# A windowed attention and feed-forward kernel whose order of operations comes from a table instead of a list scheduler

## The chip, the cores and the metric

The kernel runs on one core of a Trainium2 chip. The core has TensorE (PE in the profile, with its weight loads as PEld), VectorE (DVE), ScalarE (ACT), GpSimd (POOL) and SyncE (SP), each with a queue of its own that is worked off strictly in order, and 16 DMA engines that move what the queues issue. The metric is the time of one execution in microseconds (us), the median of three runs; lower is better.

## The reference, cut to what matters

```python
# attention: 8 batches, 8 heads, 512 local and 32 global tokens, head size 64
s_g  = scale * q_g @ concat(k_g, k_l).T          # 32 global queries see all 544 keys
out_g = softmax(s_g) @ concat(v_g, v_l)
s_ll = where(abs(i - j) <= 32, scale * q_l @ k_l.T, -1e9)
s_l  = concat(scale * q_l @ k_g.T, s_ll)         # 512 local queries: a window and the global keys
out_l = softmax(s_l) @ concat(v_g, v_l)
x = concat(out_g, out_l)  ->  4352 rows of 512
# feed-forward
h = x @ w_in                                     # 512 -> 2048
g = h * erf(softplus(h))
out = g @ w_out                                  # 2048 -> 512
```

## The kernel before

The attention goes head by head. For each pair of heads, TensorE computes the windows' scores (`s`, 64 small matmuls with 64 rows by 32 columns of the array, `scores`); VectorE adds the mask and takes the maximum (`sm`, `mx`), ScalarE takes the exponentials; TensorE transposes the result (`t`, four matmuls of 128x128); VectorE or ScalarE copies it (`pt`); TensorE multiplies it with the values (`o`, 32 small matmuls a head, 64 a pair, 128 rows by 32 columns; `va` and `vb` are the values' windows); VectorE normalizes (`rs`, `xn`). The global queries have a chain of their own (`ga`, `gb`, `gt`, `go`, `gx`). Batch by batch the result goes through DRAM (`xsc`) and comes back as the feed-forward's input (`rx`, split into `xh` and `xl`).

The feed-forward works on 512-token chunks. `h` is a block of 12 matmuls (128x128 against 512 columns; high and low parts of both factors, three products). ScalarE computes softplus and erf of a few blocks at a time, each with its own table load (`gate`), VectorE multiplies and splits (`gh`, `gl`), and `op` (`project`, six matmuls each) adds up the output. The hidden dimension is cut into 8 units; three are worked first for all chunks and their sums wait in DRAM (`part`); the other five follow in the second part, for chunk pairs with a scheme of seven products of blocks (`pa` to `pd`, weights `wq`). The weights come as 64-bit floats that VectorE turns into 32-bit ones (`raw_in`, `top_in`; `raw_l_in`, `raw_out`). At the start TensorE runs fillers (`spare`), matmuls of constants whose result nobody reads.

Everything is written as operations (`Program.add`): what engines can run it and how long that takes, a key that stands for its due time, what it reads and writes. `Program.schedule` (L192) is a list scheduler: it goes through time, keeps the free buffers of every pool, and gives each engine the ready operation with the smallest key. It has terms for the switch between tile shapes (`TURN`, L57), for a limit on TensorE's small instructions in a stretch (`crowded`, L223), for the queue's ring and for fillers. The order that it returns is the order in which the operations are written into the engines' queues and in which the buffers rotate (L1490 on):

```python
CROWD, STRETCH, EVADE = 254, 4.013, 0.444
...
            for at, m in reversed(issued):
                n += m
                if at <= now - stretch:
                    break
                if n > CROWD:
                    t = max(t, at + stretch - now)
```

Of the kernel before, what the change touches and what calls it, by code (L numbers as in the profile page):

```python
# [30 lines left out]
CROWD, STRETCH, EVADE = 254, 4.013, 0.444  # L31
# [26 lines left out]
NEAR = 3.364  # L58
# [77 lines left out]

class Op:
# [3 lines left out]
class Program:  # L141
# [46 lines left out]
    def filler(self, dur, fn, heat, since, before):  # L188

        self.idle = (dur, fn, heat, since, before)  # L190

    def schedule(self):  # L192
        free = {}
        ready = {e: [] for e in self.LAT}
        until = dict.fromkeys(self.LAT, 0.0)
        events, order, now, bus = [], [], 0.0, {"SP": 0.0, "ACT": 0.0}
        line, front = sorted(self.ops, key=lambda o: o.key), 0

        def push(op):
            for e in op.ways:  # L200
                heapq.heappush(ready[e], (op.key, op.seq, op))

        def elsewhere(op, e):

            for o, dur in op.ways.items():
                if o != e and dur < op.ways[e]:
                    wait = max(0.0, until[o] - now)
                    wait += sum(i[2].ways[o] for i in ready[o] if i[:2] < (op.key, op.seq) and i[2].eng is None)
                    if wait + dur < BIAS * op.ways[e]:
                        return True  # L210
            return False

        for op in self.ops:
            for b in op.new:
                free[b.pool, b.tag] = b.bufs - MORE.get(b.tag, 0)
            if op.waits == 0:
                push(op)
        heapq.heappush(events, (0.0, -1, 0, None))
        ahead = AHEAD
        fill_dur, fill_fn, fill_heat, since, before = self.idle  # L220
        warmth, issued, ring, mode = [], [], [], "F"

        def crowded(n):  # L223

            t = 0.0
            stretch = LOADED[2] if LOADED[0] <= now < LOADED[1] else STRETCH
            for at, m in reversed(issued):
                n += m
                if at <= now - stretch:
                    break  # L230
                if n > CROWD:
                    t = max(t, at + stretch - now)
                    break
            return t

        def fill():
            nonlocal mode
            dur = fill_dur if now > COLD else 2 * fill_dur
            until["PE"] = max(since, now) + dur
            heapq.heappush(events, (until["PE"], -1, 0, None))  # L240
            if now >= since:
                op = Op()
                op.eng, op.ways, op.fn, op.key, op.start, op.heat = "PE", {"PE": dur}, fill_fn, 0.0, now, fill_heat
                op.new, op.bufs = [], []
                order.append(op)
                warmth.append((now, fill_heat))
                mode = "F"

        taken = []

        def cools():

            return not taken and (now < COLD or now < FILL and sum(h for t, h in warmth[-200:] if t > now - TICK) < HEAT)

        while events or any(o.eng is None for o in self.ops) and ahead < 1e3:
            if not events:
                ahead *= 1.25
                heapq.heappush(events, (now, -1, 0, None))
            now = events[0][0]
            while events and events[0][0] <= now:  # L260
                _, _, kind, op = heapq.heappop(events)
                if kind == 2:
                    push(op)
# [1303 lines left out]
```

## Time and profile before

| what | value |
|---|---|
| median of 3 runs | 898.65 us (898.58 to 901.54) |
| profiled execution, from its first to its last instruction | 900.1 us |
| TensorE busy | 882.4 us, 98% |
| VectorE busy | 688.3 us, 76% |
| ScalarE busy | 549.8 us, 61% |
| mean granted clock of TensorE | 0.996 |

A row's idle time is what its engine waited just before it, and the name behind `<-` is what came last. "issue" is time in which the engine waited for nothing that the profile shows. A matmul's row overlaps the next one's, so the start of the next row tells how long one holds the engine.

### The profile page before, as it was taken

The page shows a single profiled execution, that of the slowest core. Times are in us where ns is not written, and L with a number is a line of the kernel's source. Part 1 is how long each engine was busy: PE and PEld are TensorE (multiplying, and loading weights), DVE is VectorE, ACT ScalarE, POOL GpSimd, SP SyncE. Part 2 cuts the span into 40 slices and gives each one's busy share as a digit, 9 for nine tenths or more (in the row PEclk, how much of TensorE's full clock was granted, in tenths as well). Part 3 has the DMA queues.
Part 4 walks back from the last instruction along what each step waited for, and adds up shares of the span by engine and source line. Part 5 has one row for each costly group of instructions (what it writes and reads, how often), then busy time and mean ns, then how long its engine had stood idle before and what let it go on. Part 6 is the DMA issues. An engine that isn't in the chain of part 4 may idle for free.

```text
span 900.1 us, 22151 instructions
## 1 busy us (share of the span) xinstructions
PE 882.4 (98%) x8781; PEld 717.2 (80%) x8789; DVE 688.3 (76%) x1839; ACT 549.8 (61%) x948; POOL 0.9 (0%) x5
## 2 busy tenths in 40 slices
PE   8899899999999999999999999999999999999998
PEld 4677777777877888888888888888888888888986
DVE  6898998999999978978598987587555956456443
ACT  5588866885588746854564865456524654455660
POOL 0000000000000000000000000000000000000000
PEclk9999999999999999999999999999999999999999
DMA  9898798799788948368676528444393435435222
GB/s 322 293 294 293 267 301 301 257 306 320 265 273 286 313 132 281 105 239 277 213 249 202 178 69 269 164 119 151 108 279 102 134 114 176 146 93 171 75 78 70
DMA packets 120063, 186.43 MB, mean 207 GB/s; under 512 B 14104, under 2 KB 57624, under 8 KB 119960
## 3 DMA queue, kind: packets, MB, share of 16 engines
q1 hardware_dynamic: 119960, 185.02, 62.9%
q8 instruction: 69, 1.13, 0.5%
q14 instruction: 34, 0.28, 0.1%
HBM read 143.56 MB, written 41.42 MB: 206 GB/s over the span
## 4 chain that ended last, share of the span: by engine, by line
PE 88%; DVE 6%; DMA 2%; issue 2%; ACT 1%; SPq 1%; DVEq 0%; ACTq 0%
PE op L398 40%; PE h L398 10%; PE pd L398 7%; PE pc L398 7%; PE pa L398 7%; PE pb L398 3%; PE o L398 3%; PE t L399 3%; PE s L398 3%; DVE sm L410 2%; PE h_g L398 2%; PE gt L399 1%; PE go L398 1%; PE ga L398 1%; DMA k<-in_qk_dram 1%
## 5 line engine op out<-in xcount | busy, mean ns | idle before, releaser
L398 PE MATMUL op<-wouth,gh 128*128 128x512 f32 x544 | 214.8, 395 | 0.0
L398 PE MATMUL op<-wouth,gl 128*128 128x512 f32 x544 | 211.9, 390 | 0.0
L398 PE MATMUL op<-woutl,gh 128*128 128x512 f32 x544 | 211.9, 389 | 0.0
L401 ACT ACT_TABLE_LOAD x105 | 134.7, 1283 | 2.6 <-PEq L1554 0.7
L398 PEld LDWEIGHTS op<-wouth,gh 128*128 128x128 f32 x544 | 102.1, 188 | 21.5 <-issue 0.6
L398 PEld LDWEIGHTS op<-wouth,gl 128*128 128x128 f32 x544 | 102.1, 188 | 21.5
L398 PEld LDWEIGHTS op<-woutl,gh 128*128 128x128 f32 x544 | 102.2, 188 | 20.0
L410 DVE TENSOR_TENSOR gl<-sp,gh 128x512 fp32r<-128x512 f32 x136 | 91.2, 685 | 19.6 <-PE op L398 16.0
L400 ACT ACTIVATE gh<-sp 128x512 fp32r<-128x512 f32 x67 | 42.0, 631 | 100.7 <-PE op L398 91.4
L400 ACT ACTIVATE sp<-sp 128x512 f32<-128x512 f32 x136 | 76.0, 621 | 0.5
L410 DVE CAST gh<-sp 128x512 fp32r<-128x512 f32 x69 | 28.6, 421 | 55.3 <-PE op L398 54.9
L410 DVE CUSTOM_DVE_ANT_0 sm<-s,msk 128x128 f32<-128x128 f32 x256 | 57.1, 285 | 17.3 <-PE s L398 17.2
L398 PE MATMUL h<-xh,winh 128*128 128x512 f32 (+1 forms) x168 | 67.0, 399 | 0.0
L398 PE MATMUL pa<-xh_x_B,wq 128*128 128x512 f32 x184 | 63.9, 389 | 0.0
L398 PE MATMUL pd<-xh_ih_T,wq 128*128 128x512 f32 x184 | 63.8, 389 | 0.0
L398 PE MATMUL h<-xh,winl 128*128 128x512 f32 (+1 forms) x168 | 63.2, 376 | 0.0
L398 PE MATMUL h<-xl,winh 128*128 128x512 f32 (+1 forms) x168 | 63.1, 376 | 0.0
L410 DVE TENSOR_TENSOR pair<-u,pc 128x512 f32<-128x512 f32 x46 | 31.4, 683 | 32.9 <-PE pc L398 32.8
L400 ACT ACTIVATE sm<-sm,mx 128x128 f32<-128x128 f32 x120 | 37.4, 394 | 9.1 <-DVE mx L410 9.1
L399 PE MATMUL t<-cs,sm 128*128 128x128 f32 x256 | 39.2, 286 | 3.0 <-DVE rs L410 1.1
L398 PE MATMUL o<-va,pt 128*32 128x65 f32 x768 | 37.8, 222 | 4.2 <-issue 3.5
L400 ACT ACTIVATE pt<-t 128x512 f32<-128x512 f32 x52 | 30.0, 600 | 17.8 <-PE t L399 17.7
(160 smaller groups left out, 1687.9 us busy)
## 6 DMA issues: line engine op xcount, KB each, us to landing
wq<-wq SPq DMA_DIRECT2D x161, 256.0 KB, 3.4
vb<-in_vB_dram SPq DMA_DIRECT2D x64, 325.0 KB, 5.6
qk<-in_qk_dram SPq DMA_DIRECT2D x28, 656.0 KB, 5.9
rx<-xsc SPq DMA_DIRECT2D x26, 512.0 KB, 6.0
va<-in_vA_dram SPq DMA_DIRECT2D x64, 195.0 KB, 5.3
wq<-part SPq DMA_DIRECT2D x47, 256.0 KB, 4.5
part<-os SPq DMA_DIRECT2D x34, 256.0 KB, 3.3
os<-part SPq DMA_DIRECT2D x34, 256.0 KB, 4.2
```

The source lines that it names most:

```text
L398: pe = lambda n, *a, **k: pinned(nc.tensor.matmul(n, *a, **k))
L399: tr = lambda *a, **k: pinned(nc.tensor.transpose(*a, **k))
L400: act = lambda *a, **k: pinned(nc.scalar.activation(*a, **k))
L401: table = lambda name: pinned(nc.scalar.preload_act_table_set(name))
L410: return lambda *a, **k: pinned(f(*a, **k))
```

## The change

`Program.schedule` and its constants' use go. In their place stands a string `ORDER` of 3098 words; a word is the number of an operation in the order in which they were added, with an `a` where ScalarE runs what VectorE could run too, and `w` is a filler. `Program.ordered` reads it word by word.

```diff
+ORDER = """
+w w w 53 54 349 376 348 3 59 314 318 352 4 w w w 1 316 55 56 315 61 w 2 405 w 353 317 w w 321 334 w 57a 58 354 60 w w
...
     def filler(self, dur, fn, heat, since, before):

-        self.idle = (dur, fn, heat, since, before)
-
-    def schedule(self):
...
+        self.idle = fn
+
+    def ordered(self):
+        order = []
+        for word in ORDER.split():
+            if word == "w":
                 op = Op()
...
+                op.eng, op.fn, op.new, op.ways = "PE", self.idle, [], {"PE": 0.22}
+            else:
+                op = self.ops[int(word.rstrip("a"))]
+                op.eng = "ACT" if word.endswith("a") else next(e for e in op.ways if e != "ACT" or len(op.ways) == 1)
+            order.append(op)
+        assert len({id(op) for op in order}) == len(order) and all(op in order for op in self.ops[-3:])
         return order
...
+                held_by += PIECE.values()
...
-                    need = [Q, K, PIECE[n, 0], PIECE[n, 1]]
+                    need = [Q, K, *(PIECE[i, j] for i in range(n + 1) for j in range(2))]
...
-    for op in prog.schedule():
+    for op in prog.ordered():
```

SyncE's queue at the program's start, before and then after (`q` and `k` are queries and keys of head pairs, numbered by the first head; `cs` and `mby` constants; `raw_in` pieces of `w_in` as 64-bit floats):

```order
L402 DMA cs<-in_cst_dram 128x194
L402 DMA q_0_109<-in_qk_dram 128x288
L402 DMA k_0_110<-in_qk_dram 128x416
L402 DMA q_0_109<-in_qk_dram 128x256
L402 DMA k_0_110<-in_qk_dram 128x352
L402 DMA mby<-in_cst_dram 128x128
L402 DMA q_2_120<-in_qk_dram 128x544
L402 DMA k_2_123<-in_qk_dram 128x768
L402 DMA raw_in_2_0_126<-in_w_in_dram 128x512
L402 DMA raw_in_2_1_130<-in_w_in_dram 128x512
```

```order
L378 DMA raw_in_2_0_109<-in_w_in_dram 128x512
L378 DMA k_2_113<-in_qk_dram 128x768
L378 DMA q_4_115<-in_qk_dram 128x544
L378 DMA q_2_117<-in_qk_dram 128x544
L378 DMA raw_in_2_1_120<-in_w_in_dram 128x512
L378 DMA k_0_123<-in_qk_dram 128x352
L378 DMA mby<-in_cst_dram 128x128
L378 DMA k_0_123<-in_qk_dram 128x416
L378 DMA q_0_122<-in_qk_dram 128x288
L378 DMA k_6_177<-in_qk_dram 128x768
L378 DMA q_0_122<-in_qk_dram 128x256
L378 DMA cs<-in_cst_dram 128x194
```

The weights and the second head pair's keys moved to the front, the first pair's pieces and the constants behind them.

VectorE's queue at the program's start, before and then after (`sm` and `mx` are the masked scores and their maximum, `top_in` the weights' conversion):

```order
L410 ISA sm_0_177,mx_0_178<-s_0_0_137,msk 128x128
L410 ISA mx_0_178 128x1
L410 ISA sm_0_177,mx_0_178<-s_0_0_137,msk 128x128
L410 ISA mx_0_178 128x1
L410 ISA sm_1_181,mx_1_182<-s_0_1_138,msk 128x128
```

```order
L386 TENSOR_SCALAR top_in_2_0_165<-raw_in_2_0_109 128x512
L386 SCALAR_TENSOR_TENSOR top_in_2_0_165<-raw_in_2_0_109,top_in_2_0_165 128x512 x2
L386 SCALAR_TENSOR_TENSOR top_in_2_0_165<-winh_2_111,top_in_2_0_165 128x512
L386 TENSOR_SCALAR top_in_2_1_171<-raw_in_2_1_120 128x512
L386 SCALAR_TENSOR_TENSOR top_in_2_1_171<-raw_in_2_1_120,top_in_2_1_171 128x512 x2
L386 ISA sm_2_180,mx_2_181<-s_2_0_125,msk 128x128
```

The conversion of the first two weight pieces, which stood behind the first pair's masks, comes first of all.

TensorE's queue in the third batch's attention, where the scores of the head pair from head 2 of batch 3 (`s_3_2`) stand; before and then after:

```order
L398 MATMUL s_3_2_0_2219<-qk_3_2_2058 32x128 x4
L398 MATMUL s_3_2_1_2220<-qk_3_2_2058 32x128 x4
L398 MATMUL s_3_2_0_2219<-qk_3_2_2058 32x128 x4
L398 MATMUL s_3_2_1_2220<-qk_3_2_2058 32x128 x4
L398 MATMUL h_0_1_1_2257<-xh_0_1_0_1764,winh_0_0_910 128x512
```

```order
L375 MATMUL t_2_3_2085<-cs_75,sm_2_3_1559 128x128 x4
L374 MATMUL s_3_2_0_2094<-qk_3_2_1948 32x128 x4
L374 MATMUL s_3_2_1_2095<-qk_3_2_1948 32x128 x4
L374 MATMUL s_3_2_0_2094<-qk_3_2_1948 32x128 x4
L374 MATMUL s_3_2_1_2095<-qk_3_2_1948 32x128 x4
L374 MATMUL s_3_2_0_2094<-qk_3_2_1948 32x128 x4
L374 MATMUL s_3_2_1_2095<-qk_3_2_1948 32x128 x4
L374 MATMUL s_3_2_0_2094<-qk_3_2_1948 32x128 x4
L374 MATMUL s_3_2_1_2095<-qk_3_2_1948 32x128 x4
L374 MATMUL o_2_2_2131<-va_2_2_1753,pt_2_2_1898 32x65
L374 MATMUL o_2_2_2131<-vb_2_2_1768,pt_2_2_1898 32x65 x2
```

Before, a block `h` followed these scores; now the 64 small matmuls of `o_2_2` and `o_2_3` follow them at once.

## Rows read from the trace of the kernel before

**Rows 1.** Busy time by stage: PE, PEld, DVE, ACT, POOL, clock, DMA share, GB/s.

```profile
0.00:45.00 45.00, 37.81 (x826) 24.55 (x834) 33.48 (x146) 26.10 (x65) 0.94 (x5) 0.96 0.86 308
45.00:90.00 45.00, 42.38 (x1013) 32.51 (x1012) 42.00 (x191) 36.84 (x92) 0.00 (x0) 1.00 0.89 293
90.00:150.00 60.00, 57.02 (x1093) 45.54 (x1092) 54.23 (x203) 46.08 (x102) 0.00 (x0) 0.97 0.85 286
150.00:240.00 90.00, 89.33 (x1606) 71.37 (x1605) 86.64 (x320) 61.05 (x112) 0.00 (x0) 1.00 0.90 294
240.00:395.00 155.00, 154.56 (x1987) 126.06 (x1986) 139.18 (x418) 109.02 (x189) 0.00 (x0) 1.00 0.68 228
395.00:900.10 505.10, 501.29 (x2268) 417.16 (x2266) 332.75 (x567) 270.68 (x392) 0.00 (x0) 1.00 0.51 159
```

**Rows 2.** Chain of waits, its last long piece: start us, us, what.

```profile
850.02 43.56 PE op L398 x192
```

**Rows 3.** TensorE's longest waits: us in total, times, longest us.

```profile
PE o L398 <- issue: 5.8, 6, 2.3
PE s L398 <- DMA k<-in_qk_dram: 1.4, 1, 1.4
PE s L398 <- issue: 1.2, 2, 1.0
PE t L399 <- DVE rs L410: 1.1, 1, 1.1
PE spare L398 <- PEq L1554: 0.8, 1, 0.8
```

**Rows 4.** Timeline of TensorE at two issue gaps: start, us, operation, idle before.

```profile
66.72 0.87 PE L398 MATMUL s<-qk 64*32 64x128 f32 x40
68.61 0.53 PE L398 MATMUL s<-qk 64*32 64x128 f32 x20 [1.02 <-issue]
...
97.83 0.22 PE L398 MATMUL o<-vb,pt 128*32 128x65 f32 x1 [2.27 <-issue]
```

**Rows 5.** Busy time between three issue gaps, with instruction counts.

```profile
68.00:97.80 29.80, 26.01 (x634) 20.11 (x635) 27.12 (x122) 25.16 (x59) 0.00 (x0) 1.00 0.91 312
97.80:147.50 49.70, 49.02 (x888) 39.42 (x888) 45.06 (x166) 36.44 (x74) 0.00 (x0) 0.97 0.81 270
```

**Rows 6.** DMA queues of the page: the instruction queue's packets and MB.

```profile
q8 instruction: 69, 1.13, 0.5%
```

**Rows 7.** Busy time in the two stretches of half granted clock.

```profile
29.98:33.39 3.41, 3.19 (x35) 2.54 (x38) 1.66 (x4) 2.02 (x6) 0.00 (x0) 0.50 1.05 406
98.24:101.66 3.42, 3.42 (x17) 3.42 (x18) 3.37 (x9) 1.51 (x4) 0.00 (x0) 0.50 1.01 395
```

**Rows 8.** Timeline of TensorE: `s` before another shape, `s` before the same.

```profile
159.25 1.16 PE L398 MATMUL s<-qk 64*32 64x128 f32 x64
160.34 0.55 PE L399 MATMUL gt<-cs,pg 128*128 128x128 f32 x3
...
168.28 1.16 PE L398 MATMUL s<-qk 64*32 64x128 f32 x64
169.18 1.06 PE L398 MATMUL ga<-qk 64*32 64x480 f32 x8
```

**Rows 9.** Busy time in the start's loads; the last column is GB/s.

```profile
2.00:10.00 8.00, 7.84 (x143) 3.75 (x145) 1.78 (x16) 2.63 (x9) 0.00 (x0) 1.00 0.93 277
10.00:13.00 3.00, 2.95 (x49) 2.05 (x32) 2.62 (x5) 1.74 (x4) 0.00 (x0) 1.00 1.04 407
```

**Rows 10.** Timeline of the start, TensorE and VectorE.

```profile
5.55 0.88 PE L398 MATMUL s<-k,q 64*32 64x128 f32 x32
...
7.52 0.29 DVE L410 CUSTOM_DVE_ANT_0 sm<-s,msk 128x128 f32<-128x128 f32 x1 [7.52 <-PE s L398]
...
10.28 0.43 DVE L410 TENSOR_SCALAR top_in<-raw_in 128x512 int32<-128x512 int32 x1 [0.98 <-DMA raw_in<-in_w_in_dram]
...
13.87 0.28 DVE L410 CUSTOM_DVE_ANT_0 sm<-s,msk 128x128 f32<-128x128 f32 x1
```

More of the change, by code (lines that the diff above doesn't have):

```diff
@@ new lines @@
+1124 1561 1526 1151 1565 1109a 214 1521 1566 1100 1101 1522 1593 1052 1554 1104 1527a 1159 215 1184 1102a 1162 1110
+1594a 1128 1132 1121 1193 1551 1163 1111 1112 1549a 1164 1113 101 1165 1133 1114 1595 1149 1115 1523 1194 1116 1550
+1125 1596 1134a 1150a 1170 1513 1209 1210 1187 1555a 1152a 1153 1211 1212 1213 1195 1053 1562a 1224 1154 1126 1093
+1127 1166 109 113 1214 1215a 1160 1196 1168 1597 1167 1188 1189 1155a 1156 1157 1197 1198 1190 1199a 1117 1171 1556
+1216 1135 1249 1518 1227 1235 1236 1217a 1172 219 1191 114 1139 1140 115 117 1185 1598 110 1601 1118 116 1161 1192a
@@ new lines @@
+1352 1657 1333 1335 237 238 240 1336 1337 1309 241 1310 1652a 1663 1661 225 1353 1706 1338 1707a 1703 1799 1306 1307
+1308 1623 1624 1614 1311 1670 1312 1635 1313 1354 1802a 1704 1705 233 1636 1708 234 1658 244 1630 1804 1806 1640 1800
+242 243 1631 1803 239 1807 1808 1667 1662a 1811a 1812 1826 1817 1709 1710 1738 1740 1673 1739 1741 1805 1742 1625
+1575a 1715 1671a 1750 1641 1576 1716 1717a 1809a 1637 1638a 1751 1626 1627 1628a 1664 1680 1665a 231 1823 1813a 1743
+1668a 1841 1847 1810 1818a 1712 1822 1713 1674 1675a 1677 1632 1633a 1711a 1814 1815a 235 1669 1666 1642 1752 1688
@@ new lines @@
+2350 2322 2172 2487a 2503 2324 2469 2180 2174 2325 2182 2473 2175 2360 2477a 2504 2183 2326 2475 2188 2478 2368 2365
+2190 2196 2336 2373 2339 2191 2376 2342 2353 2198 2343 2488 2345 2199 2346 2384 2489 2505 2381 2490 2348 2349 2351
+2492 2389 2491a 2354 2506 2352 2361 2357 2521 2392 2369 2377 2385 2494 2355 2356 2358 2507 2522 2359 2393 2362 2508a
+2523 2396 2399 2370 2493 2402 2378 2495 2496 2498 2497 2524 2386 2499 2525 2509 2394 2397a 2395 2511 2398 2526 2510
+2405 2513 2512 2527 2363 2514 2542 2371 2379 2387 2406 2515 2400 2409 2403a 2517 2401 2543 2404 2516 2528 2418 2544
@@ new lines @@
+2983 2815 2811a 2816 2818 2817 2984 2827 2819 2985 2708 2975a 2989 2976 2829 2843a 2846a 2844 2833 2977a 2990 2847
+2978 2854 2685 2991 2979 2693 2701 2709 2835 2849 2850 2852a 2686 2855 2992 2858 2828a 2861 2694 2830 2864 2831 2834
+2688 2702 2832a 2996 2836 2980a 2696 2689 2837 2981 2704 2697 2839 2853 2997 2838 2705 2874 2840 2998 2879 2867 2882
+2887 2710 2895 2890 2856 2712 2857 2875 2859 2713 2868 2898 2860 2871 2883 2862 2865a 2863 2891 2866 2903 2906 2899
+2986 2869 2870 2872 2876 2873 2987 2884 2988 2999 3003 3004 2907 3005 2892 2910 2913 2900 2916 2993 2908 2911a 2909
@@ L137 @@
+2967 2961 2954 2969 2962 2971 2970 2972
+"""
 class Op:
```

254 lines of the change are left out of this document (103 added, 151 removed).

## The prediction

> **What bounds the kernel now.** I read the table by stage first [rows 1]: stage less TensorE's busy time is its idle time. From 150 us on that is 0.67 us (150 to 240), 0.44 us (240 to 395) and 3.81 us (395 to the end), nearly all of this last at the very end: the chain of waits finishes with 192 `op` matmuls back to back in 43.56 us, 0.227 us each [rows 2], and what follows them is an addition and the output's transfer. So behind 150 us TensorE is the bound and nearly full. Before it the picture differs: 7.19 us idle up to 45 us, 2.62 us from 45 to 90, 2.98 us from 90 to 150. So what a better order can win as idle time, if the end stays, is 7.19 + 2.62 + 2.98 + 0.67 + 0.44 = 13.9 us of 900.1. VectorE is the second queue: 42.00 of 45, 54.23 of 60, 86.64 of 90 us [rows 1]; what TensorE waits for in these stages mostly passes through it.
>
> The list of TensorE's waits says what the idle time is [rows 3]: 5.8 us before `o` and 1.2 us before `s` are "issue", no engine and no transfer being late; 1.4 us are the keys' load and 1.1 us a VectorE operation. The two largest issue gaps lie *inside* an operation, in the middle of a row of small matmuls: 1.02 us after 40 of the 64 of an `s`, and 2.27 us inside an `o` [rows 4]. From just before the end of the first gap to just before the end of the second TensorE shows 634 matmuls and 635 weight loads, 1269 in all, which is 5 x 256 less 11; from there to the next such gap, at 147.5, 888 + 888 = 1776, 7 x 256 less 16 [rows 5] (waits on semaphores are instructions too and are not in these counts). The instruction queue moved 69 packets, 1.13 MB, so 16 KB each [rows 6]. I read this as TensorE's program arriving in pieces of 256 instructions, and a gap as a piece that came late because the piece before it, full of small matmuls, was used up too fast while the data queues were busy.
>
> The Trainium skill, "Runtime: NRT & Kernel Launch", section "Instruction fetch mechanics", says the sequencer refills in 16 KiB blocks of 256 instructions, which the rows agree with, and that crossing such a boundary is mostly hidden, which the gap of 2.27 us contradicts. By that rule the fetch term below would be nothing and the sum -5.3 us instead of -7.9 us.
>
> The granted clock fell to half twice, for 3.41 and 3.42 us, the second right behind the gap of 2.27 us [rows 4, 7]. At half clock TensorE loses half of the stretch, so 1.7 us each.
>
> **The change, part by part.** The operations are the same; 47 fillers (`spare`) stand in both programs. The two edits beside the table make the second half of the first scores, and the operations that share their `q` and `k`, wait for all the pieces of that load. I put that at 0: TensorE reaches them behind ten fillers at the start, and the bytes, worked out below, come later than that wait by themselves. On all queues the last part is word for word the same: 368 of 759 TensorE operations, and what VectorE, ScalarE and SyncE have beside and behind them. In the trace of before this part begins at 394.8 us on TensorE and within 2 us of it on the others. The last 505.1 us are therefore taken as they are, 501.29 us of them busy [rows 1], and the term is 0. What would have to go wrong is a product's weights (`wq`) or a gated tile arriving late because the first part ended earlier; queue share there is 0.51 [rows 1], so I put 0 with a bound of +2 us.
>
> *Turns of TensorE between tile shapes.* An `s` of 64 matmuls followed by `ga` (same 64*32 tiles) holds TensorE from 168.28 to 169.18, 0.90 us; the same `s` followed by the 128*128 transposes `gt` from 159.25 to 160.34, 1.09 us [rows 8]. The difference, 0.19 us, is one turn. I counted turns over the whole list of TensorE's operations (tiles 64*32 for `s` and `ga`, 128*32 for `o` and `go`, 128*128 for the rest): 140 before, 125 after, among them 13 directly from `s` to `o` where there were 2. Fifteen turns at 0.19 us are 2.9 us; at two thirds of that, since an `s` to `o` turn is not in the rows and may cost more than the average, 1.9 us. I take -2.3 us.
>
> *The start.* SyncE now issues first a piece of `w_in` (128 x 512 of 8 bytes, 524 KB), then `k` (393 KB) and two `q` (279 KB each); the scores that come first are those of heads 2 and 3 and need these 1475 KB. The load of before began to move at about 2 us and ran at 277 GB/s until 10 us and at 407 GB/s after [rows 9], so the first scores can start at 2 + 1475/277 = 7.3 us, where they start at 5.55 us now [rows 10]: 1.75 us later. Those of heads 0 and 1 need all of 3128 KB: 2216 KB by 10 us, the rest by 12.3 us, 6.7 us later than now. On the other side VectorE, which now begins at 7.52 us with these scores [rows 10], has its first weights at 2 + 524/277 = 3.9 us; the 3.6 us of weight conversion that stood between the masks of two head pairs (10.28 to 13.87 us [rows 10]) lie before the scores. For the queue that the start waits for, that is 3.6 - 1.75 = 1.9 us won if the pairs' order does not matter. From the waits of [rows 3] that are not "issue" (13.9 us less 7.0 of issue and 0.8 before the first instruction, so 6.1 us) a longer distance between a head's scores and its transposes should take some: in the median the work that TensorE has between them goes from about 9 to about 13 us, priced in the same way as the pieces below. Start and waits together: between -6.1 us (all gone) and +6.7 us (the whole delay of heads 0 and 1 shows); I take -3.0 us, nearer to the lower end since the delay is one pair's and its place is taken by another's.
>
> *Work that changes its engine.* 69 copies and scalings go from VectorE to ScalarE and 66 the other way, so of VectorE's 1236 operations three go. In each stage ScalarE has more free time than VectorE (36.84 against 42.00 of 45 us, 61.05 against 86.64 of 90 [rows 1]), and which copy stands where decides only how soon a TensorE operation is released. Its own term is 0; what it does is part of the waits' -3.0 us, whose bounds hold for it.
>
> *The pieces of the program.* The old scheduler keeps TensorE from issuing more than 254 small matmuls in 4.013 us; the table does not: behind `s_3_2` follows `o_2_2` at once, 128 + 128 instructions in about twice 0.90 us [rows 8]. That sounds as if more pieces would come late. But a piece boundary falls somewhere into such a bunch and the rest of each piece is dense `h` or `op` work: priced with the shortest rows of each operation, the shortest pieces take 3.2 us after and 3.4 us before; under 4.02 us are nine after, five of them at the start, and five before. So I expect the 7.0 us of issue gaps to stay between 4 and 10 us. The piece that ended in the 2.27 us gap becomes 0.9 us longer, and the half clock behind it should go: -0.9 - 1.7 = -2.6 us. Bounds: -7.0 - 3.4 = -10.4 us, and +3.0 us plus two more half-clock stretches, +6.4 us.
>
> *Sum.* -2.3 - 3.0 - 2.6 = -7.9 us. Against the profiled execution 900.1 - 7.9 = 892.2 us. Its span alone is 1.45 us above the median of the runs shown, 898.65 us; taken off that median the change gives 890.75 us. I say **891 us**, 0.85% faster.
>
> **Rivals.**
> 1. *What is won is lost at the same place.* The start's delay (+1.75 us on the first scores, up to +6.7 us on the first pair) eats the waits that go, and gaps for program pieces appear elsewhere at the old size. Then only the turns remain, -2 us at most: 896 to 899 us. For it: nine short pieces instead of five, and a busy start. Against it: the waits in [rows 3] have single causes that another order can avoid.
> 2. *Nearly all idle time goes.* 13.9 us of idle, less the 0.8 us before the first instruction, 3.4 us of clock loss and 2.3 us of turns: at most 18.8 us. Two thirds of it, 12.5 us, would give 886 us, all of it 880 us. For it: the distance between producer and consumer grows throughout. Against it: the start is limited by bytes, as worked out above.
> 3. *Slower: the bunches starve TensorE.* The bunches come where the queues are 0.85 to 0.90 busy, up to 240 us, and 0.68 behind [rows 1]. If each of the 11 new `s`-to-`o` bunches has a gap of 1.0 us (the smaller row of [rows 4]) and one in three is followed by a half-clock stretch, 11 + 4 x 1.7 = 17.8 us are added, less 5.3 us of turns and waits: +12.5 us, 911 us. It decides (+4.5 us) from 0.3 us a bunch on. Against it: a bunch holds 256 instructions, so it always spans two pieces, each with several us of dense matmuls.
>
> **How the numbers follow.** My forecast, between 885 and 894, has 0.51; rival 1 (894 to 903) 0.21; rival 2 (878 to 885) 0.17; rival 3 (over 903) 0.11. The likeliest one's own range is 885 to 894 us. For 8 in 10 I take the range from 881 us, where two thirds to all of the idle time would be gone, to 901 us; below it lie about 0.07 and above it 0.13 (rival 3 and the end of rival 1). A measurement of this kernel tells about 0.5% from no change, 4.5 us: faster means under 894.2 us, which is my forecast and rival 2, with 0.68; rival 1 lies within 0.5%, 0.21; slower than 903.1 us is rival 3, 0.11.
>
> **What would show it.** In the profile after: the stages up to 150 us should hold 5 to 8 us less idle time of TensorE in the same work, and from the operation that stood at 395 us on the same 505 us should follow; if that part is longer, the term 0 was wrong. The first scores should start at about 7.3 us and the first `top_in` on VectorE at about 4 us. The "issue" sum should be 4 to 10 us; above 12 us rival 3 is right. One half-clock stretch or none behind 45 us; if there are three or more, the clock term has the wrong sign. The forecast is wrong in its core if TensorE's idle sum up to 395 us is not lower than 13.9 us.

## The result and the profile after

The changed kernel takes 907.5 us in the median of four runs (904.7 to 908.02); the kernel before, beside it, 899.01 us. The ratio is 1.0081, with a 95% interval of 1.0062 to 1.0100: 0.8% slower, where 0.85% faster was forecast. In a second set of six runs it was 905.18 us, ratio 1.0064 (1.0045 to 1.0083). The profiled execution of the first set is the shortest of its four, 904.7 us with a span of 902.2 us, so the traces of before and after differ by only 2.1 us in span. Other traces of both programs, below, show more.

The stages of the changed kernel, in the columns of [rows 1]:

```profile
0.00:45.00 45.00, 33.45 (x838) 21.98 (x853) 32.36 (x143) 27.57 (x68) 0.94 (x5) 1.00 0.77 289
45.00:90.00 45.00, 42.93 (x945) 32.96 (x934) 42.86 (x181) 37.98 (x98) 0.00 (x0) 1.00 0.89 302
90.00:150.00 60.00, 59.01 (x1227) 47.64 (x1204) 58.49 (x214) 53.42 (x118) 0.00 (x0) 1.00 0.91 300
150.00:240.00 90.00, 87.15 (x1631) 70.37 (x1629) 83.56 (x308) 60.26 (x120) 0.00 (x0) 1.00 0.85 272
240.00:395.00 155.00, 151.54 (x1912) 124.51 (x1911) 142.68 (x425) 106.52 (x185) 0.00 (x0) 0.99 0.72 238
395.00:902.20 507.20, 503.39 (x2277) 418.89 (x2276) 334.71 (x571) 269.97 (x391) 0.00 (x0) 1.00 0.51 159
```

TensorE's idle time up to 395 us is 11.55 + 2.07 + 0.99 + 2.85 + 3.46 = 20.9 us, against 13.9 us in [rows 1]. By the prediction's own last sentence it was wrong in its core. Two stages got better, 45 to 90 and 90 to 150 us; the first got worse by 4.4 us, and the two that had been full by 2.2 and 3.0 us.

TensorE's longest waits, as [rows 3]:

```profile
PE s L374 <- DMA q<-in_qk_dram: 5.6, 1, 5.6
PE o L374 <- issue: 3.0, 4, 0.9
PE pa L374 <- issue: 1.9, 1, 1.9
PE go L374 <- issue: 1.3, 1, 1.3
...
PE op L374 <- DVE gl L386: 0.6, 1, 0.6
```

The largest wait is at the start, on a load. The gaps without a visible releaser sum up to about as much as before, but one of them stands before `pa`, the first of the seven-product blocks, where no row of before had a wait.

The start, in the order of time on TensorE, VectorE and ScalarE, as [rows 10]:

```profile
4.23 0.43 DVE L386 TENSOR_SCALAR top_in<-raw_in 128x512 int32<-128x512 int32 x1 [4.23 <-DMA raw_in<-in_w_in_dram]
...
7.84 1.96 PE L374 MATMUL s<-k,q 64*32 64x128 f32 x64 [5.63 <-DMA q<-in_qk_dram]
...
9.00 0.43 DVE L386 TENSOR_SCALAR top_in<-raw_in 128x512 int32<-128x512 int32 x1 [2.08 <-DMA raw_in<-in_w_in_dram]
9.46 1.42 DVE L386 SCALAR_TENSOR_TENSOR top_in<-raw_in,top_in 128x512 int32<-128x512 int32 x2
...
9.64 0.63 ACT L376 ACTIVATE msk<-mby 128x512 f32<-128x512 uint8 x1 [3.43 <-DMA mby<-in_cst_dram]
...
10.80 0.28 DVE L386 CUSTOM_DVE_ANT_0 sm<-s,msk 128x128 f32<-128x128 f32 x1
```

The first scores start at 7.84 us (7.3 was forecast) and the first conversion at 4.23 us (4 was forecast). What the forecast left out is in the last four rows. In VectorE's queue the conversion of the second weight piece stands ahead of the first mask; its `raw_in` comes at 9.0 us, after 2.08 us without work, and the conversion holds VectorE until it masks at 10.80 us. And every masked score needs `mby`, a load of 66 KB that now stands behind 2.2 MB of others and lands at 9.6 us; what ScalarE makes of it is there at 10.27 us. So VectorE masks first 3.3 us later than in [rows 10], although the scores came only 2.3 us later. The granted clock, too, becomes full later: at 11.5 us, where it was 6.1 us before, and the first 64 matmuls of `s` took 1.96 us, against 1.16 us in [rows 8].

The place of the wait before `pa`, on TensorE and in SyncE's queue (the middle row issues three loads; that of `wq0_0_3_0`, which `pa` reads, is the second of them):

```profile
356.29 0.41 SPq L378 DMA_DIRECT2D wq<-wq  x1
356.75 7.54 SPq L378 DMA_DIRECT2D raw_out<-in_w_out_dram  x2
...
372.64 1.46 SPq L378 DMA_DIRECT2D wq<-wq  x3
...
376.56 0.39 PE L374 MATMUL op<-wouth,gl 128*128 128x512 f32 x1
378.87 0.47 PE L374 MATMUL pa<-xh_x_B,wq 128*128 128x512 f32 x1 [1.92 <-issue]
```

The load is issued at 373.1 us. From 368 to 380 us the view of the transfers has, as median time from issue to landing in its last column:

```profile
wq<-wq SPq DMA_DIRECT2D x6, 256.0 KB, 5.7
```

That gives 378.8 us, and `pa` starts at 378.87, having been free to start at 376.95: 3.8 us of lead for a transfer of 5.7 us. Behind the wait the granted clock falls to half; the busy times of that stretch:

```profile
380.18:383.59 3.41, 3.41 (x10) 2.64 (x9) 3.27 (x7) 3.38 (x6) 0.00 (x0) 0.50 0.84 291
```

### The profile page after: what moved, and what is told of

Same layout as the page of the kernel before. It is cut to its first block, busy times and chain, and to the rows that moved or that the text cites. A ratio compares the mean times of both kernels' runs of the same rounds, so it can differ in the third digit from the quotient of the medians.

```text
span 902.2 us, 22144 instructions
## 1 busy us (share of the span) xinstructions
PE 877.5 (97%) x8779; PEld 716.4 (79%) x8789; DVE 694.7 (77%) x1834; ACT 555.7 (62%) x975; POOL 0.9 (0%) x5
## 4 chain that ended last, share of the span: by engine, by line
PE 78%; DVE 10%; DMA 5%; ACT 5%; issue 2%; SPq 0%; DVEq 0%; ACTq 0%
PE op L374 36%; PE pa L374 7%; PE pd L374 7%; PE pc L374 7%; PE h L374 6%; PE pb L374 3%; PE s L374 2%; PE o L374 2%; PE t L375 2%; PE h_g L374 2%; DMA rx<-xsc 1%; DVE sm L386 1%; ACT L377 1%; DVE xn L386 1%; PE go L374 1%
## 5 line engine op out<-in xcount | busy, mean ns | idle before, releaser
L374 PEld LDWEIGHTS op<-wouth,gl 128*128 128x128 f32 x544 | 102.5, 188 | 22.8 <-DVE gl L386 1.0
L374 PEld LDWEIGHTS op<-wouth,gh 128*128 128x128 f32 x544 | 102.5, 188 | 20.9 <-ACT pt L376 1.0
L386 DVE TENSOR_TENSOR pair<-u,pc 128x512 f32<-128x512 f32 x46 | 31.4, 683 | 32.7 <-PE pc L374 32.6
L374 PEld LDWEIGHTS pa<-xh_x_B,wq 128*128 128x128 f32 x184 | 34.5, 188 | 9.5 <-issue 2.3
L374 PEld LDWEIGHTS pd<-xh_ih_T,wq 128*128 128x128 f32 x184 | 34.5, 188 | 7.2
```

Of the source, the lines that this page charges most:

```text
L374: pe = lambda n, *a, **k: pinned(nc.tensor.matmul(n, *a, **k))
L386: return lambda *a, **k: pinned(f(*a, **k))
```

## Experiments

To compare traces in the same work, I took for each of the 712 real TensorE operations the median time from its start to the next one's start in the trace of before, by its kind and the next one's tile shape. The sum over the operations ahead is "the work done"; an operation's start less that sum is how far TensorE is *behind* the work (fillers count as no work). It grows with every wait, filler and half-clock stretch. The table holds it where 40, 100, 340 and 380 us of work are done and near the end (860), in us, with the times of all runs against the kernel before. The places 340 and 380 enclose the wait before `pa`.

| run | behind at 40 | 100 | 340 | 380 | 860 | median us | ratio (95%) |
|---|---|---|---|---|---|---|---|
| before | 22.2 | 28.6 | 33.2 | 33.2 | 33.3 | 899.0 | |
| e13, before again | 21.9 | 26.9 | 31.5 | 31.5 | 31.6 | 899.88 | 0.9996 (0.9980–1.0013) |
| changed kernel | 25.8 | 27.2 | 30.2 | 34.8 | 34.9 | 907.5 | 1.0081 (1.0062–1.0100) |
| e0, changed again | 25.9 | 29.9 | 33.3 | 38.5 | 38.6 | 905.18 | 1.0064 (1.0045–1.0083) |
| e1, two loads exchanged | 26.3 | 27.6 | 33.0 | 34.8 | 35.7 | 904.39 | 1.0049 (1.0031–1.0068) |
| e4, loads sorted | 25.5 | 27.4 | 31.9 | 32.6 | 33.3 | 903.05 | 1.0042 (1.0025–1.0060) |
| e2, late part old | 25.9 | 28.1 | 48.0 | 48.0 | 48.4 | 919.48 | 1.0219 (1.0196–1.0242) |
| e3, start old | 20.5 | 26.9 | 30.9 | 33.8 | 33.9 | 906.15 | 1.0065 (1.0044–1.0087) |
| e5, start old, sorted | 21.3 | 28.9 | 32.4 | 32.8 | 33.4 | 903.48 | 1.0040 (1.0024–1.0056) |
| e7, VectorE +16 copies | 26.8 | 30.9 | 38.0 | 41.1 | 41.1 | 908.08 | 1.0091 (1.0072–1.0110) |
| e8, sorted, VectorE lighter | 26.6 | 28.3 | 31.2 | 31.5 | 31.6 | 902.02 | 1.0027 (1.0014–1.0041) |
| e9, before, VectorE lighter | 19.6 | 22.8 | 25.5 | 25.5 | 25.6 | 897.65 | 0.9979 (0.9961–0.9996) |
| e10, k and q first | 24.7 | 26.1 | 30.0 | 31.6 | 32.6 | 904.15 | 1.0046 (1.0026–1.0066) |
| e11, fillers first | 24.4 | 28.0 | 30.2 | 31.0 | 31.8 | 902.75 | 1.0040 (1.0022–1.0058) |
| e12, start by need | 26.0 | 27.6 | 31.3 | 31.8 | 32.6 | 903.75 | 1.0041 (1.0018–1.0063) |
| e15, start by need, cs too | 28.0 | 30.2 | 33.5 | 34.1 | 35.1 | 904.8 | 1.0064 (1.0042–1.0086) |
| e14, first part old, sorted | 22.0 | 28.8 | 35.4 | 36.0 | 36.9 | 903.63 | 1.0042 (1.0025–1.0059) |

Not shown is e6 (953.77 us). The traces of one and the same program differ by 1.7 us (before) and 3.7 us (changed) at the end, so single traces tell apart only what is larger, or a wait that is there or not.

**The changed kernel again (e0).** No edit.

> The changed kernel once more, as the base of the experiments, with a second trace. Its four runs spread from 904.7 to 908.0 us and the trace is of the shortest; the other three had spans 3 to 4 us longer. Late-weights theory (the loss is made between 370 and 385 us, where the first product pa waits 1.9 us for weights and the clock halves behind it): a longer run shows longer waits there, by 2 to 4 us. Start theory (the loss is the first scores' delay of about 5.8 us at 14 us): a longer run shows the extra in the first 75 us. Piece theory (issue gaps): the issue sum is 10 us or more in a longer run, against 7.3 us.

Its trace is 3.7 us longer. The wait before `pa` is there again with 1.9 us, with 1.1 us before an `op` for `gl` and one half-clock stretch; between 340 and 380 us of work it falls back by 5.2 us, the first trace by 4.6 us. That is the same loss in both. The extra of the longer run lies elsewhere, mostly between 80 and 100 us of work, so no theory had its place; two issue gaps, of 0.9 and 1.3 us at 111 and 117 us, are most of it.

**Two loads exchanged (e1).** 1820 is the load of `wq0_0_3_0`, 1827 is `pa`, 1826 the load of `wq3_0_3_0`, which is needed later:

```diff
-1662a 1811a 1812 1826 1817 1709
+1662a 1811a 1812 1820 1817 1709
...
-1758 1718 1845 1820 1827 1689
+1758 1718 1845 1826 1827 1689
```

> The changed kernel with two words of its table exchanged: the load of wq0_0_3_0, which stands right before its product pa_0_3_0, takes the place of the load of wq3_0_3_0, which stands 150 words before its product. Nothing else moves. Late-weights theory: the wait of 1.9 us before pa goes and the half-clock stretch behind it (1.7 us) too, so 3.6 us less than the changed kernel, about 904 us, and no new wait of more than 0.5 us before the late wq3. Start theory and piece theory: no change, 907 to 908 us.

TensorE's waits from 335 to 460 us:

```profile
PE pa L374 <- DVE c L386: 0.9, 1, 0.9
PE pc L374 <- DVE c L386: 0.6, 1, 0.6
PE op L374 <- DVE gl L386: 0.3, 1, 0.3
```

The wait of 1.9 us and the half clock are gone: the load's place made the wait. For the half clock that is less certain, since e3 has the wait without it. But 2.7 us came back behind it (33.0 to 35.7 in the table), 1.8 us of them in waits for VectorE. In the time only 0.8 us are left, within the uncertainty.

**All fourteen loads sorted (e4).** The loads' words in the table's order, one line before and one after; their places stay:

```diff
-1826 1823 1841 1847 1822 1821 1845 1820 1842 1824 1844 1825 1843 1846
+1820 1822 1821 1823 1824 1841 1825 1826 1842 1843 1844 1845 1846 1847
```

> The changed kernel, with the 14 loads of the first two products' weights (wq0 to wq6 of 0_3_0 and 0_3_1) put into their 14 places in the order in which TensorE needs them. Late-weights theory in its first form (only the order of these loads is wrong): the whole 4.6 to 5.2 us that the two traces of the changed kernel lose between 340 and 395 us go, about 901 us. Late-VectorE theory (the exchange of two loads alone gave back 2.6 us in waits for VectorE's c, since VectorE is filled there by conversions that the table put off): the same waits of 0.5 to 1 us come again, 903 to 905 us.

Its stages up to 395 us, and the sum over the span:

```profile
0.00:45.00 45.00, 34.11 (x842) 21.84 (x850) 32.34 (x142) 27.45 (x68) 0.94 (x5) 1.00 0.80 289
45.00:90.00 45.00, 43.36 (x924) 32.81 (x905) 42.33 (x179) 37.47 (x96) 0.00 (x0) 1.00 0.87 298
90.00:150.00 60.00, 57.33 (x1160) 46.56 (x1165) 58.02 (x213) 52.51 (x118) 0.00 (x0) 1.00 0.89 299
150.00:240.00 90.00, 87.34 (x1627) 70.33 (x1628) 83.17 (x302) 60.45 (x120) 0.00 (x0) 1.00 0.83 268
240.00:395.00 155.00, 153.36 (x2015) 126.68 (x2005) 143.84 (x432) 108.19 (x187) 0.00 (x0) 1.00 0.74 244
...
sum 900.60, PE 877.00 PEld 715.37 DVE 694.46 ACT 555.62 POOL 0.94; mean PE 146.17 PEld 119.23 DVE 115.74 ACT 92.60 POOL 0.16
```

TensorE's waits from 335 to 460 us:

```profile
PE op L374 <- DVE gl L386: 0.4, 1, 0.4
PE pc L374 <- DVE c L386: 0.3, 1, 0.3
```

Between 340 us of work and the end it now loses 1.4 us instead of 4.7 and 5.3. In the time it is 903.05 us, 2.1 us under e0 and 4.5 us under the first set; its interval and that of e0 overlap, so the size in the time is less certain than the wait in the trace. That leaves 3.1 us to the kernel before.

**The late part in the order of before (e2).** From the 300th TensorE operation on, all that is left stands in the order of before:

```diff
-1597 1167 1188 1189 1155a 1156 1157 1197 1198 1190 1199a 1117 1171 1556
+83 127 129 132 1645 1646 103 105 1647 106 1518 110a 1552a 1553
```

> The changed kernel's table up to its 300th TensorE operation (about 279 us in its trace); from there all that is left stands in the order of before. Late-weights theory: the waits between 370 and 385 us (0.55 + 1.9 + 1.7 us) go and the 2.4 us that the middle had gained stay: span about 898, time about 900 us. Start theory: the start's loss stays whole, 905 to 908 us. Piece theory: 904 to 908 us, since the gaps up to 279 us stay.

The first row of TensorE's waits:

```profile
PE t L375 <- ACT sm L376: 13.9, 2, 12.0
```

This is TensorE's longest wait in that trace (total, times, longest). All three theories missed: 919.48 us. The loss is at the cut, where VectorE and ScalarE first work off what the old order had behind them by then, and TensorE waits 12.0 us in one piece. Behind the cut, from 280 us of work to the end, this trace loses 0.5 us: the old order of the late part has no wait of its own.

**The start in the order of before (e3, and e5 with sorted loads).** What stands ahead of the 120th TensorE operation is put into the order of before:

```diff
-w w w 53 54 349 376 348 3 59 314 318 352 4
+4 3 0 314 315 316 317 w 318 w 1 w w 348
```

> The operations that the changed kernel's table has before its 120th TensorE operation (about 77 us) stand in the order of before; the rest of the table stays. Late-weights theory: the first scores come 2 us earlier again, but the two traces stand within 1 us of each other at 75 us in the same work, so the time stays within 1.5 us of the changed kernel, 906 to 908.5 us. Start theory: 4 to 6 us less, 902 to 904 us. Piece theory: issue gaps of this part go back to those of before, 1 to 2 us less.

> Both edits at once: what stands before the 120th TensorE operation in the order of before, and the 14 weight loads in the order of need. If start and weights are lost independently: 901 us less what the start is worth, 899 us or less. If the start's 5 us are given back by 100 us whatever its order (as the trace with the old start shows: 20.5 against 25.8 us behind the work at 40 us of it, 26.9 against 27.2 at 100), it equals the run with the sorted loads alone within 2 us.

At 40 us of work they are 5.3 and 4.2 us ahead of the same table with the new start, at 100 us no more than 0.3 ahead, and at the end within 1 us; 906.15 and 903.48 us. I first read that as a start that is given back whatever its order. The waits of e3 from 45 to 100 us say otherwise:

```profile
PE s L374 <- ACT pt L376: 2.7, 2, 2.0
```

They stand just before the cut at 77 us (e5: 2.8 us), and e2 shows what a cut can cost. So these two runs don't tell whether the start matters.

**The start without a cut (e10, e11, e12, e15).** All on the sorted loads. The first words of the table, changed, then in e10, in e12 and in e15 (349 and 348 are `k` and `q` of heads 2 and 3, 314 to 318 those of heads 0 and 1, 1 is `mby`, 0 is `cs`, 53 and 59 are `raw_in`); e11 only moves twelve fillers of the changed kernel's own start, ten ahead of the first scores and two right behind them.

```diff
-w w w 53 54 349 376 348 3 59 314 318 352 4 w w w 1 316 55
+w w w w w w w w w w 349 348 1 3 4 2 352 w w 353 354 53 54 376
...
+w w w w w w w w 349 348 1 314 318 316 315 317 3 4 2 352 w w 353
...
+w w w w w w w w 349 348 1 0 314 318 316 315 317 3 4 2 352 w w 353
```

> On the kernel with the sorted weight loads: SyncE issues k_0_2, q_0_2 and the mask mby first and raw_in behind them, VectorE masks the scores of heads 2 and 3 before it converts the first weights, and 12 of the 47 fillers stand ahead of and right behind these scores. Nothing else moves, so there is no seam. By bytes the scores can start at 2 + 672/277 = 4.4 us (7.84 us in the changed kernel), the first masked score at about 6 us (10.80 us). Start theory (what the changed order has lost against before, apart from the weights, is its start: 5.6 us of wait for q and a cold clock until 11.5 us): 3 to 5 us less than 903.05, so 898 to 900 us. Theory that a start's gain is given back by 100 us: 902 to 904 us.

> On the kernel with the sorted weight loads: only 12 of the 47 fillers move, ten of them ahead of the first scores, where TensorE waits for q anyway. The granted clock should be full before 7.84 us instead of from 11.5 us, so the first 64 scores take about 0.9 us instead of 1.96. Start theory: 1 to 1.5 us less, 901.5 to 902 us. Theory that the first masked score waits for mby (landed at 9.6 us) and not for the scores: no change, 903 us.

> On the kernel with the sorted weight loads: SyncE issues k and q of heads 2 and 3, the mask mby, then all of k and q of heads 0 and 1, and only then raw_in and q_0_4; VectorE masks these heads before it converts weights; 10 fillers stand in front. TensorE's order of real work stays. By bytes the second pair's scores start at 2 + (672 + 66 + 672)/277 = 7.1 us. Start theory: TensorE's DMA waits in the first 45 us fall from 6.9 to under 2.5 us and the time falls from 903 by 3 to 5 us, to 898 to 900 us. If the middle is what loses: the waits fall and the time stays at 902 to 903.5 us.

> As the run with the start's loads by need, and cs (99 KB) loaded right behind the mask. Start theory: no DMA wait over 1 us in the first 45 us, TensorE's idle time there at most 7.5 us as before (10.2 us with cs late), and the time 2.5 to 3.5 us lower, 900 to 901 us. Middle theory: the wait goes and is given back by 100 us, 902.5 to 904 us.

The longest wait of the start in each trace, as the timeline of TensorE has it. In e11, with the loads as they were, it is still for `q` of heads 2 and 3:

```profile
7.19 1.96 PE L374 MATMUL s<-k,q 64*32 64x128 f32 x64 [2.73 <-DMA q<-in_qk_dram]
```

In e10, with these heads' loads first, it is for `q` of heads 0 and 1:

```profile
10.77 0.79 PE L374 MATMUL s<-k,q 64*32 64x128 f32 x32 [4.30 <-DMA q<-in_qk_dram]
```

In e12 it is for `cs`, at the first transposes:

```profile
14.93 0.88 PE L375 MATMUL t<-cs,sm 128*128 128x128 f32 x4 [3.05 <-DMA cs<-in_cst_dram]
```

In e15 it is for ScalarE's exponentials, at the same transposes:

```profile
15.27 1.20 PE L375 MATMUL t<-cs,sm 128*128 128x128 f32 x4 [2.61 <-ACT sm L376]
```

Each load that is brought forward uncovers the next wait. With all of them forward (e15) TensorE's idle time in the first 45 us is 7.84 us, near the 7.2 us of [rows 1], but the trace has two half-clock stretches there, and the time, 904.8 us, is no better. In e11 the clock was full from 3.6 us and half again from 7.0 to 10.4 us, behind the 2.73 us without work, so the scores took 1.96 us as before. Theories of the start got none of their 3 to 5 us; that the start is the rest of the loss is not shown. The theory on record against them, that the middle loses, had the waits gone and the time at 902 to 904 us; in e15, where no wait for a load is over 1 us, it is a little above that.

**VectorE heavier and lighter (e7, e8, e9).** e7 puts 16 copies into the changed table between the 72nd and the 142nd TensorE operation; e8 (on the sorted loads) and e9 (the kernel before) leave out one step of each weight conversion, so that the three lowest bits of a weight are missing:

```diff
+            elif word == "v":
+                op = Op()
+                op.eng, op.fn, op.new, op.ways = "DVE", self.extra, [], {"DVE": 0.35}
...
+    prog.extra = lambda: dve.tensor_copy(extra, MSK.ap.rearrange("p t k -> p (t k)")[:, :256])
```

```diff
-            dve.scalar_tensor_tensor(top, word(0), 29, top, op0=ALU.logical_shift_right, op1=ALU.bitwise_or)
```

> The changed kernel with 16 copies of 128x256 more on VectorE (nobody reads their result), spread evenly over the VectorE operations that stand between the 72nd and the 142nd TensorE operation (46 to 99 us). By the 128x256 casts at 0.28 us and the 128x512 copies at 0.68 us they hold VectorE for 5 to 6 us. If VectorE bounds the first 100 us: TensorE reaches the same work 4 to 6 us later at 100 us. If it doesn't: under 1.5 us there. Whether it shows at the end says whether the stretch from 150 to 340 us can take back a delay: 906 us if it can, 910 to 912 us if not.

> The changed kernel with the weight loads in the order of need, and one step fewer on VectorE in each conversion of a weight piece: the third of four, which brings in the three lowest bits, is left out (0.69 us each; 9 pieces stand before the 100th TensorE operation, 23 before the last 368). VectorE theory (up to 340 us VectorE, 92 to 96% busy, decides, so no order of TensorE's work can gain there): TensorE reaches the same work 3 to 6 us earlier at 100 us and 5 to 10 us earlier at 340 us, and the time falls from 903 to 894 to 899 us. If TensorE's own turns and program pieces or the loads decide: within 1.5 us of 903.

> The kernel before, its order untouched, with the same step of each weight conversion left out. VectorE theory, in the form that both orders run against VectorE alike: it gains as much as the changed order does, 4 to 8 us, 892 to 896 us. If the changed order gained TensorE time that VectorE only hides, the changed order gains at least 3 us more from the lighter VectorE than this one. If VectorE decides only in the changed order: 899 to 900 us, no change.

The copies of e7, by their tile (count, shortest, median and longest in ns), took less than forecast, 16 x 0.286 us = 4.6 us with their overlap still in it:

```profile
L389 DVE COPY extra<-msk x16: 250/286/292, 47.3 to 97.9; 128x256 f32<-128x256 f32 x16
```

At 100 us of work TensorE is 3.7 and 1.0 us later than in the two traces of the changed kernel (4 to 6 were forecast), at 340 us 7.8 and 4.7 us. It ends 2.9 us above e0 but only 0.6 us above the first set, and the intervals overlap, so what of it shows in the time is not settled. Its counterpart does not bear the theory out. In e8 VectorE's busy time over the span falls from 694.46 (e4) to 674.46 us:

```profile
sum 898.90, PE 876.81 PEld 715.30 DVE 674.46 ACT 556.18 POOL 0.94; mean PE 146.13 PEld 119.22 DVE 112.41 ACT 92.70 POOL 0.16
```

At 100 us of work TensorE is no earlier (28.3 against 27.4 us behind) and the time falls by 1.0 us only; the kernel before gains 2.3 us (its trace shows more, but is one of its shortest executions, 894.54 us of 894.18 to 902.97). That VectorE holds the changed order back falls with it, in the form that was on record (3 to 6 us at 100 us). What the lighter VectorE does mend is the late part: between 340 us of work and the end e8 loses 0.4 us, e4 1.4 us.

**The engines of before (e6).** Each of the 135 operations that changed its engine goes back; the order stays:

```diff
-w 337 338a 351 w 377
+w 337 338 351 w 377
```

> The changed kernel's order, but each of the 135 copies and scalings that changed its engine goes back to the engine of before. If the swaps are worth nothing (my prediction): 904 to 908 us as the changed kernel. If VectorE's 6 us more busy time up to 397 us (361.6 against 355.3 us) come from the swaps and count: 2 to 4 us less. If the table's order fits only its own engines: waits grow, 910 us or more.

953.77 us, ratio 1.0608 (1.0581 to 1.0636); from 240 to 395 us TensorE is busy 139.72 of 155 us:

```profile
240.00:395.00 155.00, 139.72 (x2209) 111.44 (x2208) 122.68 (x417) 85.57 (x159) 0.00 (x0) 0.98 0.66 215
```

The swaps are part of the order: each queue is in order, and an operation on the other engine stands behind other work. "Its own term is 0" was a price for something that can't be had by itself.

**The kernel before again (e13), and its first part with the rest changed (e14).** e13 has no edit; e14 has the order of before up to the 300th TensorE operation, then the changed one with sorted loads, and so begins with the words of e3.

```diff
-w w w 53 54 349 376 348 3 59 314 318 352 4
+4 3 0 314 315 316 317 w 318 w 1 w w 348
```

> The kernel before once more, for a second trace: 898 to 901 us. If its first trace stands for it: TensorE's idle time up to 395 us is again 13 to 15 us with two half-clock stretches. If that trace was of a slow run: 1 to 3 us less idle time.

> The order of before up to its 300th TensorE operation (285 us), all the rest in the changed order with the sorted weight loads. If the changed order's remaining 3 us are lost before that point (the start): 899 to 901 us. If they are lost behind it (VectorE full from 340 us, waits for gl and c): 902 to 903 us. A cut that costs several us shows as waits at 285 to 300 us.

e14 loses 4.4 us at its cut (31.6 behind at 240 us of work, 36.0 at 260) and tells nothing on the first part. e13 is the better measure of before: span 898.5 us, 14.7 us of TensorE's idle time up to 395 us (13.9 us in the first trace) and no half clock behind the start. Its stages up to 395 us and the sum over its span:

```profile
0.00:45.00 45.00, 37.63 (x828) 23.96 (x837) 34.26 (x150) 26.28 (x67) 0.94 (x5) 1.00 0.88 313
45.00:90.00 45.00, 40.22 (x1002) 30.82 (x1001) 40.01 (x174) 35.91 (x90) 0.00 (x0) 1.00 0.86 279
90.00:150.00 60.00, 58.37 (x1107) 46.08 (x1106) 56.63 (x219) 47.40 (x106) 0.00 (x0) 1.00 0.88 299
150.00:240.00 90.00, 89.42 (x1607) 71.61 (x1606) 86.89 (x322) 61.99 (x113) 0.00 (x0) 1.00 0.90 300
240.00:395.00 155.00, 154.69 (x1986) 126.41 (x1985) 138.38 (x414) 108.81 (x187) 0.00 (x0) 1.00 0.66 223
...
sum 898.50, PE 880.00 PEld 714.58 DVE 688.24 ACT 550.04 POOL 0.94; mean PE 146.67 PEld 119.10 DVE 114.71 ACT 91.67 POOL 0.16
```

Its first three waits of TensorE, all of them issue gaps:

```profile
PE o L398 <- issue: 6.1, 6, 1.6
PE s L398 <- issue: 2.1, 3, 0.9
PE x L399 <- issue: 1.4, 1, 1.4
```

And one row of SyncE's queue:

```profile
342.16 3.41 SPq L402 DMA_DIRECT2D wq<-wq  x7
```

This is the load of the first products' seven weights, issued from 342 to 346 us, and `pa` starts at 386.3 us in this trace. Before, these loads had 40 us of room; in the changed table the one that is needed first has 3.8 us.

## Why the prediction was wrong

The sum was -7.9 us; the two sets of the changed kernel measured +8.5 and +5.3 us.

**The last 505 us: right in itself, and still the step that failed.** From the first operation of the identical part (at 396.87 us) to the end of the span the changed kernel takes 505.3 us, as before. The prediction named what could go wrong, a product's weights (`wq`) arriving late, and put 0 with a bound of 2 us on it, because the queues' last parts are word for word the same. But the first of these products, and the load that feeds it, stand just ahead of that part, where the order is new: in the table the load of `wq0_0_3_0` is the word right before `pa`, while `wq3_0_3_0`, needed last, comes 78 words earlier, and SyncE is held up for 7 us behind a `raw_out` in between. The exchange of two words takes the wait away (e1), which shows the cause. All five traces of tables in which this load stands right before its reader have a wait there: 1.9 us in the first set and e0, 2.1 us in e3 and e6, 2.4 us in e7, where the profile puts it down to ScalarE. In e6 it names the load:

```profile
430.06 0.50 PE L374 MATMUL pa<-xh_x_B,wq 128*128 128x512 f32 x1 [2.06 <-DMA wq<-wq]
```

Of the tables with the load further ahead only e1 has a wait before `pa`, the 0.9 us for VectorE shown above. The size is 4.6 and 5.2 us in two traces (0.6 and 1.1 us for `gl`, 1.9 us for the weights, 1.7 us of half clock are its known parts), above the bound; e4 shows some 3.5 us of it to be the order of these loads, the rest are waits for VectorE.

**Start and waits, -3.0 us: the sign was wrong.** Compare two traces that have no half clock behind the start, e13 and e4: idle time of TensorE is span less busy, 898.5 - 880.0 = 18.5 us before and 900.6 - 877.0 = 23.6 us after, so +5.1 us with the late weights already mended. By stage, from the rows above: up to 45 us it goes from 7.4 to 10.9 us, from 45 to 90 us from 4.8 to 1.6, from 90 to 150 us from 1.6 to 2.7, from 150 to 240 us from 0.6 to 2.7, from 240 to 395 us from 0.3 to 1.6. So the start costs 3.5 us and the next stage gives 3.1 us of it back, as the table has it too: e4 is 3.6 us behind e13 at 40 us of work and 0.5 us at 100. The rest is lost behind 90 us, 3.4 us of it in the two stages that had been full. Fillers count as busy here, so these are rough sums.

The bytes of the first scores were worked out well (7.3 us, measured 7.84), but the 1.75 us were priced as a delay of one pair whose place another takes. Nothing could take it at once: the mask, the other pair's `q` and `cs` stand behind the same 2 MB, and the conversions that VectorE does early instead aren't what TensorE waits for. And the 0.67 and 0.44 us of the full stages were counted as idle time to be won; that an order could lose time there had no price in the sum. From 150 to 395 us the ten traces of changed tables without a cut have 3.1 to 8.8 us of idle time, the two of before 1.1 and 0.9 us.

**Turns, -2.3 us: right as far as the traces tell.** TensorE's busy time, fillers included, falls from 880.0 (e13) to 877.0 us (e4), -3.0 us; the medians of the operations by the next one's shape, over seven traces, give -1.3 us. The turn from `s` to `o` costs what the others do: an `s` of 64 holds TensorE 1.09 us before `o` and 0.90 us before `s`, the 0.19 us of [rows 8].

**Program pieces and clock, -2.6 us: not there.** The sum of waits named issue, up to 420 us, is 7.7 us in the trace of before and 10.3 us in e13, 7.8 in that of the changed kernel (1.9 of them the weights) and 5.5 to 9.3 in the other changed tables without a cut. It was to be 4 to 10 us, and rival 3 falls by its own mark, 12 us: the bunches of `s` and `o` don't starve TensorE. But nothing was gained either: the gaps moved. That they are program pieces is borne out by their places. Counted in the trace, 705, 961, 1218, 2242, 5315, 7361 and 11202 matmuls, weight loads and waits of TensorE stand ahead of the seven issue gaps of 0.5 us or more in e4, each 193 to 195 more than a multiple of 256. In the first trace of before the counts are 957, 2746, 3002, 4025 and 5817, and the second has the same five and three more; they are 185 to 189 over a multiple, with eight fillers missing from these records. The wait before `pa` stands at 233 and is none of them. So in these traces the order sets where a gap can be; which of the places show one, and how long, varies between executions.

In both traces of before they lie ahead of 150 us; the changed order has such places at 186 to 191 and at 295 to 303 us, in the stages that had been full, and each of the ten traces shows a gap at one or both. TensorE's issue gaps before `o` from 150 to 395 us, in the changed kernel and in e4 (none in either trace of before):

```profile
PE o L374 <- issue: 1.9, 2, 0.9
...
PE o L374 <- issue: 2.8, 2, 1.6
```

The half-clock stretches that were to go are absent from the first trace of the changed kernel, e0, e1 and e4 between the start and 380 us, but also from the second trace of before. They are not foreign to its order, though: e14, which has that order for its first 285 us, shows both again, at 29.5 and 97.7 us, and e9 the first, at 28.0 us. The prediction took the 1.02 us of [rows 4] for the second largest gap; that one is of 1.75 us and stands ahead of the first stretch:

```profile
28.20 0.22 PE L398 MATMUL o<-va,pt 128*32 128x65 f32 x1 [1.75 <-issue]
```

The Trainium skill, "Runtime: NRT & Kernel Launch", section "Instruction fetch mechanics", has boundary crossings mostly hidden. The traces agree with "mostly": of 69 pieces [rows 6], 7 to 14 a trace show a wait named issue. The one gap of 2.27 us, which the prediction set against that sentence, does not contradict it; whether an order can remove the gaps that show is not shown.

**Engine swaps, 0:** e6 shows that they can't be priced apart from the order.

Of the rivals the first, "what is won is lost at the same place", is nearest to what e4 measures: the turns are won, the start's delay eats what the next stage wins, and gaps for program pieces appear elsewhere. Its 896 to 899 us were still too low, and the late weights came on top. What is left after e4, 3.1 us in the time, is by the traces not the start: e4 is 0.4 us behind e13 at 340 us of work and 1.7 us at 860. In the five sorted tables without a cut (e4, e10, e11, e12, e15) 1.3 to 2.6 us are lost between 340 and 860 us of work, where both traces of before lose 0.1; e8, with its lighter VectorE, loses 0.4. No run took this loss away in a kernel that computes the whole, and the executions of the changed tables scatter by several us, so the cause of this rest is not settled. No version that computes the whole beats the kernel before.

## What to carry to other kernels

When two orders share their last part word for word, check where the loads that feed its first operations stand, and what blocks the queue ahead of them; a load that is written right before its reader has only the lead that its queue happens to have over the reader, here 3.8 us for a transfer of 5.7. Stages that are full can only lose: give a new order a price there, too. An order that brings the large loads forward at the start delays the small constants that every first chain needs, and mending one load uncovers the next. Gaps and half-clock stretches of one trace are a sample: look at a second trace before a term of a sum is built on them.

## What was not expected of the hardware

The half-clock stretches, 3.41 us each or a multiple (6.83 us in e6, 17.07 us in e2), come and go between executions of one program: two in the first trace of before, none in the second, though its issue gaps are larger in sum (10.3 against 7.7 us; the longest is 1.6 against 2.3 us). The wait before `pa` was followed by one in two traces (1.9 us both times) and by none in three others (2.1 us in e3 and e6, 2.4 us in e7). Gaps without a releaser stood at the same counts of instructions in two executions of a program (before and e13, the changed kernel and e0), but not all of them showed in both. And the changed tables scatter more: e11's twelve runs lie between 899.85 and 906.49 us, and those of the kernel before beside them between 897.35 and 902.2 us.
